# A score matmul with its own wait, one gate bank, and a last round in halves: attention on one Trainium2 core

## The chip, the core and the metric

The kernel runs on one core of one Trainium2 chip. The metric is the device time of an execution in microseconds; a time for a kernel is the median of several executions. Beside it stands one profiled execution, which records every instruction of every engine: TensorE (PE, its weight loads PEld), VectorE (DVE), ScalarE (ACT), GpSimd (POOL), and SyncE (SP), which issues most of the DMAs.

## What is computed

Two attentions over the same x of 2048 positions and 512 features, with 32 heads of 16, mixed by a gate of each position:

```python
x = A_x
g = _sigmoid((x * gate_w).sum(-1, keepdims=True))
a = _A_ref(x, A_wqkv, A_wo)      # softmax(q k^T / 4) v, then wo
b = _B_ref(x, B_wqkv, B_wo)      # phi(q) (phi(k)^T v) / (phi(q) sum phi(k)), then wo
return g * a + (1 - g) * b
```

Here phi(t) is t + 1 for positive t and exp(t) otherwise, and everything comes in bfloat16. The softmax branch is nearly all of the work: 32 x 2048 x 2048 scores, each of which needs an exponential.

## The kernel before

**A planner writes the order.** The kernel is a Python program that simulates the engines while it is built. In a loop (from L1394) it asks a set of functions for candidates (`cand_s`, `cand_pv`, `cand_op1`, `cand_exp` and so on, and the steps of the tasks), picks one by planned start, priority and a few constants (L160 to L184), and records it with `emit` (L308) or `dma` (L340). `_Eng.add` (L62) keeps, for each engine, the list of instructions with the semaphore values that they wait for. Then the lists are played into the program as they stand. So the order on each engine is fixed at build time, and a changed cost or constant can redraw all of it.

**Waits.** A group of PE instructions recorded together waits once, ahead of its first, and signals once, at its last. An instruction carries one wait itself; further ones become EventSemaphore instructions ahead of it on the same engine. The waits stand in the order in which the dependencies were listed, and the first one goes into the instruction itself.

**Scores.** The softmax branch has 32 rounds: four heads' positions at a time (t8, a query chunk of 512, and a parity), and within a round 16 key blocks by 4 row groups. One unit is one matmul of 32x128 weights with 512 queries, which fills one PSUM bank of 128x512. All 2048 come from `cand_s` (L614) or `cand_dsolo`. Banks 0 and 1, and 2 and 3, are ScalarE's two sets; banks 4 and 5 are VectorE's. A score wave is two matmuls for a set of ScalarE and mostly one for VectorE, as one group with one wait and one signal:

```python
fns = [s_fn(r, kb, j, b0 + k) for k, (r, kb, j) in enumerate(units)]
fns += [s_fn(u[0], u[1], j, bk) for _, j, u, bk in extra]
```

**Exponentials.** ScalarE takes a set with one exp of 128x1024 (L771) into one of ten slots of P. VectorE makes its exponentials by integer arithmetic: op1 (L685) writes scaled 16-bit integers to Z, from which two shifted versions are made, on POOL (L739) or VectorE (L749); read as bfloat16, the three are multiplied with three scaled copies of V.

**PV.** Waves of four matmuls (L775 on, `cand_pv`) add P or Z times V into bank 7. At a round's end `aout` (L1016) transposes bank 7 to T1 on VectorE (L1021), takes the reciprocal of the sums (L1040), multiplies it with the gate (L1042), scales (L1044), and transposes into OAT (L1048). In the last round the small steps are on VectorE.

**Other tasks** fill PE between: projections (`t_q`, `t_k`, `t_v`, whose scaled copies of V are POOL's L988), phi of k and q (exp L1056, L1057, L1058), the linear branch's sums and outputs, and `t_final` (L1172), which applies the two output matrices and writes 128 rows. PE is kept busy by matmuls on a dummy tile where nothing else is due (`fill`, L1347).

**The gate** is `t_gate` (L993). POOL spreads the gate weights over 128 columns (L994). For each of the four query chunks, four matmuls (each as four column groups, 64 in the trace) make the logits in a bank of its own, VectorE transposes it (L1002), and POOL picks a column of 16. Then ScalarE's exp, POOL's +1, VectorE's reciprocal into gt (used by L1042), POOL's 1-g (L1010), and four copies on VectorE (L1013) into gnat, which the linear branch's output uses. The spread weights share storage with T2 and the transposes with outt.

**SP's queue.** SP issues, in order, the loads of x and of the weights (wA: the softmax branch's, wB: the linear branch's), eight small DMAs for each query tile (Qz<-QT, within SBUF, L965), the transposing DMAs of the linear branch's output (xnat<-wA, L1168), and the writes of the output.

**The tail.** The last four `t_final` need the last round's OAT. Their copies out of PSUM are two on ScalarE (L1202) and two on VectorE (L1204).

Of the kernel before, what the change touches and what calls it, by code (L numbers as in the profile page):

```python
# [28 lines left out]
class _Ev:  # L29
    __slots__ = ("E", "idx")  # L30

    def __init__(self, E, idx):
        self.E = E
        self.idx = idx


class _Eng:
# [24 lines left out]
    def add(self, fn, deps=(), inc=True, dma_sem=None):  # L62
        waits = []
        for d in deps:
            if d is None:
                continue
# [8 lines left out]
            for k, (s2, v2) in enumerate(waits):  # L75
                if s2 is sem:
                    if val > v2:
                        waits[k] = (sem, val)
                    break
            else:  # L80
                waits.append((sem, val))
# [46 lines left out]
def bass_gated_mix__mha_block__linear_attn_block__prompt_kernel(  # L128
# [31 lines left out]
    FILL = 0.704  # L160
    HOT = 32.85
    BACK = 1005.06
    SHB = 4
    why = [None]
    PMIN = 2
# [3 lines left out]
    STICK = 45.888  # L169
    OPP = 400  # L170
    FDL = 60
    DENS = 0.581
    AGE = 300.0
    MZ = 0.0
    MZD = 0.0
    HOLD = 74.192
    NACT = 4
    BIAS = 141.142
    KEYW = 32.578
    PVW = 1365.46  # L180
    DTOL = 44.045
    TTOL = 38.407
    PKR, MTR, PQR, PQS, FR = 0.500, 9.56, 12.93, 1.804, 0.0
    KR, KS, QR = 7.15, 1.60, 4.00  # L184
# [5 lines left out]
    with ExitStack() as es:  # L190
# [40 lines left out]
        gwr = T2[:, 0, :].rearrange("p (c n) -> p c n", c=NCC)  # L231
# [10 lines left out]
        ge = SB([128, NQC, 16], FP32, "ge")  # L242
# [7 lines left out]
        PE = _Eng("pe", SEM("s_pe"), 150.0)  # L250
# [26 lines left out]
        r_OAT = [[R(f"OAT{t}_{q}") for q in range(NQC)] for t in range(NT8)]  # L277
        r_eb = [R(f"eb{i}") for i in range(2)]
# [8 lines left out]
        r_gt, r_ge, r_gl, r_gnat = R("gt"), R("ge"), R("gl"), R("gnat")  # L287
# [20 lines left out]
        def emit(E, dur, fns, reads=(), writes=(), name=""):  # L308
# [4 lines left out]
            fin = start + dur + E.pipe  # L313
# [5 lines left out]
            for k, fn in enumerate(fns):  # L319
                ev = E.add(fn, deps if k == 0 else (), inc=(k == len(fns) - 1))  # L320
                if first is None:
                    first = ev
# [11 lines left out]
            RLOG.append((E.name, dur, E.pipe, [(d.E.name, d.idx) if isinstance(d, _Ev) else ("dma", id(d.sem), d.val) for d in deps if d is not None],  # L334
# [3 lines left out]
        dma_eng = {}  # L338

        def dma(E, o, i, sem, total, lat, reads=(), writes=(), transpose=False, noncontig=False, name="dma", issue=60.0):  # L340
            start = max(E.free, _avail(E, reads, writes))
            E.free = start + issue
            fin = start + lat
            eng = {"sp": nc.sync, "act": nc.scalar, "pool": nc.gpsimd}[E.name]
# [47 lines left out]
        q_fill = [0] * NQZ  # L392
# [1132 lines left out]
```

The softmax here doesn't subtract the row's maximum and nothing guards it: scores larger than these inputs give would overflow.

## Time and profile before

| what | us |
|---|---|
| median of 8 executions | 681.16 |
| lowest and highest of them | 678.72, 681.62 |
| the profiled execution, device time | 680.91 |
| its span | 678.8 |
| ScalarE busy (share of the span) | 658.2 (97%) |
| PE busy | 666.1 (98%) |
| VectorE busy | 609.2 (90%) |
| POOL busy | 550.2 (81%) |

The span runs from the first to the last recorded instruction; 2.1 us of the device time lie around it. A row of the groups, for example

```profile
L739 POOL TENSOR_TENSOR Z<-Z,mcon 128x512 int32<-128x512 int32 x465 | 480.0, 1056 | 80.8 <-DVE Z L685 48.3
```

reads: line 739 of the kernel, on GpSimd, writes tile Z from Z and mcon, 465 times; 480.0 us in total, 1056 ns each; before these instructions the engine stood idle for 80.8 us, of which 48.3 ended when VectorE's L685 was done. Instructions of one engine overlap in part, so a mean duration can be longer than the time from one to the next, and the busy time of a group is the union. In the rows of the timeline, neighbouring instructions of a kind are put together with a count. The granted PE clock was full in all 40 slices.

### The profile page before, as it was taken

Reading aid. Unit: us, or ns where it says so; the run is one execution under the profiler, and the core shown is the slowest. Engines: PE = TensorE matmul, PEld = TensorE weight load, DVE = VectorE, ACT = ScalarE, POOL = GpSimd, SP = SyncE. Lnnn points to the kernel's source line nnn. Section 1 sums busy time; section 2 is a strip of 40 time slices with the busy share of each in tenths; the row PEclk is TensorE's granted clock in tenths of the full one; section 3 lists DMA queues with packets and bytes.
Section 4 is the critical chain, followed back from the end, with each engine's and each line's share of the span. In section 5 each row is a group of like instructions: output and inputs, shape, how many; then the busy total and the mean of one; then the engine's idle time right before and its main releaser. Section 6 shows DMA issues by size and latency. Waiting matters only on the chain.

```text
span 678.8 us, 24102 instructions
## 1 busy us (share of the span) xinstructions
PE 666.1 (98%) x9886; PEld 202.6 (30%) x9886; DVE 609.2 (90%) x1062; ACT 658.2 (97%) x734; POOL 550.2 (81%) x611
## 2 busy tenths in 40 slices
PE   8899999999999999999999999999999999999998
PEld 3322233323223232222333322232332332222222
DVE  6889999998899998999899888899998988899996
ACT  6799999999999999999999999999999998999995
POOL 4677879889878888888897888898788997887882
PEclk9999999999999999999999999999999999999999
DMA  6520001200000000000001000001020021000000
GB/s 128 138 88 6 5 2 20 85 8 4 2 9 2 10 2 2 10 2 2 12 3 65 10 10 1 10 15 24 7 34 9 14 47 33 17 16 11 26 17 32
DMA packets 27963, 15.96 MB, mean 24 GB/s; under 512 B 19792, under 2 KB 26832, under 8 KB 27856
## 3 DMA queue, kind: packets, MB, share of 16 engines
q1 hardware_dynamic: 26512, 13.91, 8.1%
q8 instruction: 79, 1.29, 0.8%
q10 hardware_dynamic: 1344, 0.52, 0.3%
q14 instruction: 28, 0.23, 0.1%
HBM read 6.69 MB, written 2.10 MB: 13 GB/s over the span
## 4 chain that ended last, share of the span: by engine, by line
PE 72%; ACT 14%; issue 5%; DVE 4%; SPq 3%; DMA 1%; POOL 0%; ACTq 0%; DVEq 0%
PE ps L371 56%; PE ps L377 17%; ACT P L771 13%; SPq L348 2%; DVE Z L685 2%; ACT eb L1056 1%; DMA gwc<-in_gate_w_dram 1%; DMA xnat<-wA 0%; DVE T L1021 0%; DVE gnat L1013 0%; DVE QT L957 0%; DVE wA L1163 0%; POOL Vc L988 0%; SPq L352 0%; DVE Z L749 0%
## 5 line engine op out<-in xcount | busy, mean ns | idle before, releaser
L771 ACT ACTIVATE P<-ps 128x1024 bf16<-128x1024 f32 x695 | 645.8, 1119 | 8.3 <-PE ps L371 8.1
L739 POOL TENSOR_TENSOR Z<-Z,mcon 128x512 int32<-128x512 int32 x465 | 480.0, 1056 | 80.8 <-DVE Z L685 48.3
L685 DVE TENSOR_SCALAR Z<-ps 128x512 int16<-128x512 f32 x659 | 440.9, 684 | 53.4 <-PE ps L371 45.3
L371 PE MATMUL ps<-Z,Vc 128*17 128x512 bf16 x1977 | 282.5, 382 | 0.3
L371 PE MATMUL ps<-Qz,KT 32*128 32x512 bf16 x2048 | 272.4, 385 | 3.4 <-DVE Z L685 1.0
L371 PE MATMUL ps<-P,Vc 128*17 128x512 bf16 x1389 | 250.2, 383 | 2.2 <-POOL Vc L988 2.1
L371 PEld LDWEIGHTS ps<-Qz,KT 32*128 32x128 bf16 x2048 | 68.7, 91 | 259.0 <-ACT P L771 234.9
L371 PEld LDWEIGHTS ps<-Z,Vc 128*17 128x17 bf16 x1977 | 63.9, 88 | 79.2 <-issue 52.3
L749 DVE TENSOR_SCALAR Z<-Z 128x1024 int16<-128x1024 int16 x195 | 82.5, 439 | 0.2
L371 PEld LDWEIGHTS ps<-P,Vc 128*17 128x17 bf16 x1389 | 56.3, 88 | 57.5 <-issue 40.6
L371 PE MATMUL ps<-warm 128*32 128x512 bf16 (+15 forms) x600 | 61.9, 326 | 1.2 <-DVE dummy L420 1.2
L377 PE MATMUL ps<-xT,wA 128*32 128x512 bf16 (+1 forms) x528 | 43.9, 376 | 0.7 <-DMA xT<-in_A_x_dram 0.4
L1057 POOL TENSOR_SCALAR eb<-eb 128x512 f32<-128x512 f32 x32 | 20.1, 629 | 15.6 <-ACT eb L1056 9.1
L988 POOL TENSOR_SCALAR Vc<-Vc 128x576 bf16<-128x576 bf16 x32 | 21.7, 679 | 6.2 <-DVE Vc L985 2.7
L371 PEld LDWEIGHTS ps<-warm 128*32 128x32 bf16 (+1 forms) x600 | 20.2, 95 | 18.6 <-issue 12.1
L1021 DVE STREAM_TRANSPOSE T<-ps 128x512 f32<-128x512 f32 x32 | 22.6, 707 | 2.5 <-PE ps L377 2.3
L377 PE MATMUL ps<-wA,xnat 128*32 128x512 bf16 x256 | 22.6, 382 | 1.8 <-DVE wA L1163 1.8
L1044 POOL TENSOR_TENSOR T<-T,rg 128x256 bf16<-128x256 f32 x31 | 19.5, 630 | 5.8 <-DVE Z L749 2.7
L377 PE MATMUL ps<-phiK,xnat 128*32 128x512 bf16 x256 | 23.2, 383 | 0.0
L1056 ACT ACTIVATE eb<-ps 128x512 f32<-128x512 f32 x32 | 22.6, 705 | 0.0
L377 PE MATMUL ps<-wA,OAT 128*32 128x512 bf16 x256 | 22.5, 382 | 0.0
L377 PE MATMUL ps<-wB,xT 128*32 128x512 bf16 x256 | 22.4, 382 | 0.0
(79 smaller groups left out, 277.3 us busy)
## 6 DMA issues: line engine op xcount, KB each, us to landing
Qz<-QT SPq DMA_DIRECT2D x120, 16.0 KB, 1.8
wA<-in_A_wqkv_dram SPq DMA_DIRECT2D x4, 384.0 KB, 4.2
wB<-in_B_wqkv_dram SPq DMA_DIRECT2D x4, 384.0 KB, 3.2
xnat<-in_A_x_dram SPq DMA_DIRECT2D x3, 512.0 KB, 3.8
out_dram<-outt SPq DMA_DIRECT2D x12, 128.0 KB, 1.7
wA<-in_A_wo_dram SPq DMA_DIRECT2D x1, 512.0 KB, 3.8
wA<-in_B_wo_dram SPq DMA_DIRECT2D x1, 512.0 KB, 4.8
out_dram<-wA SPq DMA_DIRECT2D x4, 128.0 KB, 1.8
```

The lines of the kernel that those rows point to most:

```text
L348: return eng.dma_start_transpose(o, i)
L371: return lambda: nc.tensor.matmul(o, lhsT=l, rhs=r, start=start, stop=stop, skip_group_check=sg)
L377: h = nc.tensor.matmul(o[32 * j:32 * j + 32], lhsT=l[:, 32 * j:32 * j + 32], rhs=r, start=start, stop=stop, skip_group_check=True)
L685: return C(DV, OPP, 533 * n + 74, lambda: nc.vector.tensor_scalar(o, i, ZB, 0.0, op0=ALU.add, op1=ALU.max), [r_bank[b] for b in bks], r_Z[ ...
L739: return C(PO, 400, 70 + 484 * n, lambda: nc.gpsimd.tensor_tensor(Z[:, z, 0:512 * n].bitcast(I32), Z[:, z0, 0:512 * n].bitcast(I32), mcon[ ...
L749: return C(DV, 450 if hot else 300, 69 + 134 * n, lambda: nc.vector.tensor_scalar(Z[:, z, 0:512 * n], Z[:, z0, 0:512 * n], float(m), None, ...
L771: return C(AC, 500, 427 * n + 49, lambda: nc.scalar.activation(P[:, slot, 0:512 * n], bank(b0, n), ACT.Exp, scale=ESC), [r_bank[b0 + k] fo ...
L988: yield po(690, lambda k=k: nc.gpsimd.tensor_scalar(Vc[:, k, vs].rearrange("p a b c -> p (a b c)"), Vc[:, 0, vs].rearrange("p a b c -> p ( ...
L1021: yield dv(607, lambda: nc.vector.transpose(T1[:, a, :], bank(7)), [r_bank[7]], [r_T1[a]])
L1044: yield E(340 if r == NR - 1 else 640, lambda k=k: (nc.vector if r == NR - 1 else nc.gpsimd).tensor_tensor(dst_[:, k], src[:, k, :, 0:16], ...
L1056: yield ac(480, lambda: nc.scalar.activation(eb[:, i, :], bank(b), ACT.Exp), [r_bank[b]], [r_eb[i]])
L1057: yield po(640, lambda: nc.gpsimd.tensor_scalar(eb[:, i, :], eb[:, i, :], 1.0 + 1e-6, 0.0, op0=ALU.min, op1=ALU.max), [r_eb[i]], [r_eb[i]])
```

## The change

Five things change.

1. In `cand_s` the VectorE matmul of a score wave is no longer in ScalarE's group. It is recorded as a group of its own directly behind (`part`), with its own waits and its own signal.
2. `add` sorts dependencies by the planned finish of what is waited for (`fin`), so that the order of the waits of an instruction changes.
3. `t_gate` makes the logits of the four query chunks in one bank: 16 matmuls instead of 64, one transpose instead of four, and an exp over 16 columns that reads the transposed tile itself. The result lies in another layout, so sixteen DMAs of 32x16 numbers bring it to gt, and four more bring 1-g to gnat in place of the four VectorE copies. The spread weights are 32 columns wide instead of 128.
4. In the last round `aout` works in two halves of 256 columns, each from the transpose of bank 7 to the transpose into OAT. Of the last four `t_final`, two depend on the first half and two on the second. Three of their copies are on ScalarE and one on VectorE.
5. The planner's constants have other values, and the planner counts a time for each DMA in SP's queue (1100 ns for a transposing one, 590 for a Qz one, 300 for any other).

In the order that comes out, PE has 9802 matmuls instead of 9886 (48 of them the gate's; the rest are fills), ScalarE 693 exps of 128x1024 instead of 694 and one half, VectorE 662 op1 instead of 659, and SP 201 DMAs instead of 181. On SP the sixteen gate DMAs stand behind four loads of wA and the first of wB, and ahead of the first two blocks of Qz and the other three loads of wB. The diff, with declarations left out:

```diff
@@ -61,9 +62,7 @@
         waits = []
-        for d in deps:
-            if d is None:
-                continue
+        for d in sorted([d for d in deps if d is not None], key=lambda d: d.fin if isinstance(d, _Ev) else 0.0):
             if isinstance(d, _Raw):
...
@@ -74,11 +73,10 @@
                 if s2 is sem:
-                    if val > v2:
-                        waits[k] = (sem, val)
+                    val = max(val, v2)
+                    del waits[k]
                     break
-            else:
-                waits.append((sem, val))
+            waits.append((sem, val))
         self.n += 1
...
@@ -157,31 +155,33 @@
-    FILL = 0.704
+    FILL = 0.711
...
-    BACK = 1005.06
-    SHB = 4
+    BACK = 980.186
+    SHB = 3
...
-    PMIN = 2
+    PMIN = 3
...
-    STICK = 45.888
+    STICK = 65.578
...
-    DENS = 0.581
+    DENS = 0.598
...
+    PEP = 148.771
+    PVD = 216
...
-    HOLD = 74.192
+    HOLD = 109.508
...
-    BIAS = 141.142
-    KEYW = 32.578
-    PVW = 1365.46
-    DTOL = 44.045
+    BIAS = 120.045
+    KEYW = 39.753
+    PVW = 685.579
+    DTOL = 114.55
...
-    PKR, MTR, PQR, PQS, FR = 0.500, 9.56, 12.93, 1.804, 0.0
-    KR, KS, QR = 7.15, 1.60, 4.00
+    PKR, MTR, PQR, PQS, FR = 0.404, 9.56, 12.93, 1.667, 0.0
+    KR, KS, QR = 7.15, 1.48, 4.00
...
@@ -305,12 +307,12 @@
 
-        def emit(E, dur, fns, reads=(), writes=(), name=""):
+        def emit(E, dur, fns, reads=(), writes=(), name="", more=0.0):
             if callable(fns):
...
             E.free = start + dur
-            fin = start + dur + E.pipe
+            fin = start + dur + E.pipe + more
             deps = deps_of(E, reads, writes)
...
@@ -583,10 +591,11 @@
         class C:
-            __slots__ = ("E", "prio", "dur", "fns", "reads", "writes", "after", "name", "mode", "wt", "lock", "task")
+            __slots__ = ("E", "prio", "dur", "fns", "reads", "writes", "after", "name", "mode", "wt", "lock", "task", "part")
 
...
                 self.task = task
+                self.part = None
                 self.wt = wt
...
@@ -627,10 +636,13 @@
             n = len(units)
-            reads = s_reads(units + [(u[0], u[1], j) for _, j, u, _ in extra])
+            reads = s_reads(units)
             fns = [s_fn(r, kb, j, b0 + k) for k, (r, kb, j) in enumerate(units)]
-            fns += [s_fn(u[0], u[1], j, bk) for _, j, u, bk in extra]
-            writes = writes[:n] + [r_bank[x[3]] for x in extra]
+            part = None
+            if extra:
+                part = (216.0, [s_fn(u[0], u[1], j, bk) for _, j, u, bk in extra], s_reads([(u[0], u[1], j) for _, j, u, _ in extra]),
+                        [r_bank[x[3]] for x in extra], "Dsolo" + "".join(f"+D{x[2]}{x[1]}" for x in extra))
+            writes = writes[:n]
 
...
@@ -644,8 +656,9 @@
             STATS.setdefault('sn', {})
-            return C(PE, 1000, 222, fns, reads, writes, after, f"S{units}" + "".join(f"+D{x[2]}{x[1]}" for x in extra), "row",
-                     0.25 * (n + len(extra)))
+            c = C(PE, 1000, 222, fns, reads, writes, after, f"S{units}", "row", 0.25 * (n + len(extra)))
+            c.part = part
+            return c
 
...
@@ -991,26 +1004,33 @@
-            yield po(900, lambda: nc.gpsimd.tensor_copy(gwr, gwc[:].unsqueeze(2).to_broadcast([128, NCC, 128])), [r_gw], [r_gwr])
-            yield ("WAIT", lambda: ("x", 0) in flags and phi_free[0])
-            phi_free[0] = False
+            yield po(400, lambda: nc.gpsimd.tensor_copy(gwr, gwc[:].unsqueeze(2).to_broadcast([128, NCC, 32])), [r_gw], [r_gwr])
+            yield ("WAIT", lambda: all(("x", t) in flags for t in range(NQC)))
+            b = yield ("BANK",)
+
+            def g4(cc):
+                def go():
+                    for j in range(4):
+                        h = nc.tensor.matmul(bank(b)[32 * j:32 * j + 32], lhsT=gwr[:, cc, :], rhs=xT[:, cc, 512 * j:512 * (j + 1)],
+                                             start=(cc == 0), stop=(cc == NCC - 1), skip_group_check=True)
+                    return h
+                return go
+            for h in range(2):
+                yield pe_step(2, 512, [g4(2 * h), g4(2 * h + 1)], [*[r_xT[t][h] for t in range(NQC)], r_gwr], [r_bank[b]])
+            yield dv(607, lambda: nc.vector.transpose(gl, bank(b)), [r_bank[b]], [r_gl, *r_outt])
+            yield ("FREE", b)
+            yield ac(230, lambda: nc.scalar.activation(ge[:, 0, :], gl.rearrange("p (a b) -> p a b", b=32)[:, :, 0], ACT.Exp, scale=-1.0),
+                     [r_gl, *r_outt], [r_ge])
+            yield po(150, lambda: nc.gpsimd.tensor_scalar(ge[:, 1, :], ge[:, 0, :], 1.0, None, op0=ALU.add), [r_ge], [r_ge])
+            yield dv(170, lambda: nc.vector.reciprocal(ge[:, 0, :], ge[:, 1, :]), [r_ge], [r_ge])
...
-                b = yield ("BANK",)
-                for h in range(2):
-                    yield pe_step(2, 512, [mmt(bank(b), gwr[:, cc, :], xT[:, cc, 512 * qc:512 * (qc + 1)], start=(cc == 0), stop=(cc == NCC - 1))
-                                           for cc in (2 * h, 2 * h + 1)], [r_xT[qc][h], r_gwr], [r_bank[b]])
-                yield dv(607, lambda b=b: nc.vector.transpose(gl, bank(b)), [r_bank[b]], [r_gl, *r_outt])
-                yield ("FREE", b)
-                yield po(250, lambda qc=qc: nc.gpsimd.tensor_copy(ge[:, qc, :], gl.rearrange("p (a b) -> p a b", b=32)[:, :, 0]),
-                         [r_gl, *r_outt], [r_ge])
-            phi_free[0] = True
-            yield ac(300, lambda: nc.scalar.activation(gt[:], ge[:], ACT.Exp, scale=-1.0), [r_ge], [r_gt])
-            yield po(200, lambda: nc.gpsimd.tensor_scalar(ge[:], gt[:], 1.0, None, op0=ALU.add), [r_gt], [r_ge])
-            yield dv(650, lambda: nc.vector.reciprocal(gt[:], ge[:]), [r_ge], [r_gt])
-            yield po(200, lambda: nc.gpsimd.tensor_scalar(ge[:], gt[:], -1.0, 1.0, op0=ALU.mult, op1=ALU.add), [r_gt], [r_ge])
+                for a in range(4):
+                    yield ("DMA", gt[32 * a:32 * (a + 1), qc, :], ge[32 * qc:32 * (qc + 1), 0, :], semGN, 256, 2500.0, [r_ge], [r_gt], False,
+                           qc == 0 and a == 0)
+            yield po(200, lambda: nc.gpsimd.tensor_scalar(gp[:], gt[:].rearrange("p q (c a) -> p a (q c)", a=4), -1.0, 1.0, op0=ALU.mult, op1=ALU.add),
+                     [r_gt], [r_gp])
...
-                src = ge[32 * a:32 * (a + 1), :, :].rearrange("p q (c a2) -> p (q c) a2", a2=4)[:, :, a]
-                yield dv(150, lambda a=a, src=src: nc.vector.tensor_copy(gnat[32 * a:32 * (a + 1), :], src), [r_ge], [r_gnat])
+                yield ("DMA", gnat[32 * a:32 * (a + 1), :], gp[32 * a:32 * (a + 1), a, :], semGP, 64, 2500.0, [r_gp], [r_gnat], False, a == 0)
...
@@ -1018,10 +1038,16 @@
-            yield dv(607, lambda: nc.vector.transpose(T1[:, a, :], bank(7)), [r_bank[7]], [r_T1[a]])
+            def tr_half(hf):
+                cs = slice(256 * hf, 256 * (hf + 1))
+                return dv(341, lambda: nc.vector.transpose(T1[:, a, cs], bank(7)[:, cs]), [r_bank[7]], [r_T1[a]])
+            if r == NR - 1:
+                yield tr_half(0)
+            else:
+                yield dv(607, lambda: nc.vector.transpose(T1[:, a, :], bank(7)), [r_bank[7]], [r_T1[a]])
...
-                st["acc_free"] = True
+                st["acc_free"] = r < NR - 1
...
@@ -1031,6 +1057,20 @@
+            if r == NR - 1:
+                for hf in range(2):
+                    cs, gs = slice(256 * hf, 256 * (hf + 1)), slice(8 * hf, 8 * (hf + 1))
+                    if hf:
+                        yield tr_half(1)
+                    sv = T1[:, 1, cs].rearrange("p (q d) -> p q d", d=32)
+                    yield dv(115, lambda sv=sv, gs=gs: nc.vector.reciprocal(rec[:, 1, gs], sv[:, :, 16]), [r_T1[1]], [r_rec[1]])
+                    yield dv(70, lambda gs=gs: nc.vector.tensor_tensor(rg[:, c, 1, gs], rec[:, 1, gs], gt[:, qc, gs], ALU.mult), [r_rec[1], r_gt], [r_rg[c]])
+                    yield dv(210, lambda sv=sv, gs=gs, cs=cs: nc.vector.tensor_tensor(
+                        T2[:, c, cs].rearrange("p (q h d) -> p h q d", h=2, d=16)[:, 1], sv[:, :, 0:16],
+                        rg[:, c, 1, gs].unsqueeze(2).to_broadcast([128, 8, 16]), ALU.mult), [r_T1[1], r_rg[c]], [r_T2[c]])
+                    yield dv(341, lambda cs=cs: nc.vector.transpose(OAT[:, t8, 512 * qc:512 * (qc + 1)][:, cs], T2[:, c, cs]), [r_T2[c]], [r_OATL[hf]])
+                    yield ("FLAG", lambda hf=hf: flags.add(("oatl", hf)))
+                return
...
@@ -1038,10 +1078,9 @@
             yield dv(155 + 17 * n, lambda: nc.vector.reciprocal(rc, src[:, :, :, 16]), rT1, rr)
-            E = dv if r == NR - 1 else po
-            yield E(70 if r == NR - 1 else 230 + 25 * n, lambda: (nc.vector if r == NR - 1 else nc.gpsimd).tensor_tensor(rgc, rc, gv, ALU.mult), [*rr, r_gt], rrg)
+            yield po(230 + 25 * n, lambda: nc.gpsimd.tensor_tensor(rgc, rc, gv, ALU.mult), [*rr, r_gt], rrg)
             for k in range(n):
-                yield E(340 if r == NR - 1 else 640, lambda k=k: (nc.vector if r == NR - 1 else nc.gpsimd).tensor_tensor(
+                yield po(640, lambda k=k: nc.gpsimd.tensor_tensor(
                     dst_[:, k], src[:, k, :, 0:16], rgc[:, k].unsqueeze(2).to_broadcast([128, 16, 16]), ALU.mult),
...
@@ -1185,10 +1224,10 @@
-                return [r_xn[qb], r_woB] if kind == "b" else [r_OAT[i][qc], r_woA]
+                return [r_xn[qb], r_woB] if kind == "b" else [r_OATL[qbl // 2] if tail and i == NT8 - 1 else r_OAT[i][qc], r_woA]
...
-            yield ("WAIT", lambda: ("oat", NT8 - 1, qc) in flags)
+            yield ("WAIT", lambda: (("oatl", qbl // 2) if tail else ("oat", NT8 - 1, qc)) in flags)
...
@@ -1198,7 +1237,7 @@
                 yield ("WAIT", lambda: qb < 2 or ("f", qb - 2) in flags)
-            if tail and qbl % 2 == 1:
+            if tail and qbl != 2:
                 yield ac(480, lambda: nc.scalar.copy(ot, bank(b)), [r_bank[b]], [r_ot])
...
@@ -1450,13 +1489,17 @@
-                fin = dma(SP, o, i, sem, tot, lat, reads=rd, writes=c.writes, transpose=tr, name=c.name)
+                fin = dma(SP, o, i, sem, tot, lat, reads=rd, writes=c.writes, transpose=tr, name=c.name, occ=1100.0 if tr else 590.0 if c.name[0] == 'Q' else 300.0)
...
-                fin = emit(c.E, c.dur, c.fns, c.reads, c.writes, name=c.name)
+                if c.part:
+                    emit(PE, 6.0, c.fns, c.reads, c.writes, name=c.name, more=c.dur - 6.0)
+                    fin = emit(PE, c.part[0], *c.part[1:4], name=c.part[4])
+                else:
+                    fin = emit(c.E, c.dur, c.fns, c.reads, c.writes, name=c.name)
```

## The prediction

> **What bounds the kernel now.** I read the busy shares first, then the groups by line and form, then the waits, and then walked the timeline along every gap of ScalarE.
>
> ```profile
> PE 666.1 (98%) x9886; PEld 202.6 (30%) x9886; DVE 609.2 (90%) x1062; ACT 658.2 (97%) x734; POOL 550.2 (81%) x611
> ...
> L771 ACT ACTIVATE P<-ps 128x1024 bf16<-128x1024 f32 x694 | 645.3, 1120 | 8.3 <-PE ps L371 8.1
> L685 DVE TENSOR_SCALAR Z<-ps 128x512 int16<-128x512 f32 x659 | 440.9, 684 | 53.4 <-PE ps L371 45.3
> ```
>
> PE has the larger share, but its ends are modelled and part of its work is filling (600 matmuls on `warm`), so its 98% says little. ScalarE is the bound: 694 exps of 128x1024 with 8.3 us idle before them in the whole span. Their durations (1120 ns) overlap; what counts is from one end to the next, 917 ns in the steady stretches. 694 x 0.917 is 636 us, and the 32 exps of the linear branch (L1056) add 0.49 each. What exceeds 917 ns sums to about 10.2 us, and that is all a better order can win, unless exps go away.
>
> ```profile
> PEld ps L371 <- ACT P L771: 238.0, 602, 1.2
> ...
> ACT P L771 <- PE ps L371: 8.1, 7, 4.1
> ...
> PEld ps L371 <- DVE Z L685: 13.9, 55, 0.5
> ```
>
> These are waits: total us, times, longest. PE waits for the exp to free its banks 602 times: the loop is exp, score matmuls, exp, with ScalarE last. Only 55 times does the score wave end its wait on VectorE. ScalarE waits on PE 7 times, 4.1 us in one of them.
>
> The 10.2 us, found on the timeline (start, duration, and in brackets the idle time before):
>
> ```profile
> 23.40 0.61 POOL L994 COPY T<-gwc 128x512 bf16<-128x512 bf16 x1 [2.75 <-DMA gwc<-in_gate_w_dram]
> ...
> 25.67 0.40 PE L371 MATMUL ps<-P,Vc 128*17 128x512 bf16 x4 [2.06 <-POOL Vc L988]
> ...
> 26.12 4.03 ACT L771 ACTIVATE P<-ps 128x1024 bf16<-128x1024 f32 x4 [4.05 <-PE ps L371]
> ```
>
> The gate's weight copy waits for its DMA, POOL's Vc scaling is behind it, PE's PV wave behind that, the exp behind that: 4.9 us at 21 to 27 us.
>
> ```profile
> 64.06 2.13 DVE L1013 COPY gnat<-ge 32x16 f32<-32x16 f32 x4
> ...
> 67.27 0.40 PE L371 MATMUL ps<-Qz,KT 32*128 32x512 bf16 x3 [1.03 <-DVE Z L685]
> ```
>
> Four gate copies hold VectorE 2.1 us; the score wave then waits for its bank, and the exp at 67.70 is 0.86 late. A third place is 562 us: 1.9 us, behind the transposes that follow eight Qz DMAs on the SP queue (551.8 to 557.5). Two small ones at 36 and 39 us (0.54, 0.29) stand beside the gate's matmuls; the start costs 0.6, the rest is spread.
>
> ```profile
> 36.70 5.58 SPq L352 DMA_DIRECT2D Qz<-QT  x8
> 42.32 0.58 SPq L352 DMA_DIRECT2D wB<-in_B_wqkv_dram  x1
> 43.23 2.41 SPq L352 DMA_DIRECT2D Qz<-QT  x4
> 45.68 0.58 SPq L352 DMA_DIRECT2D wB<-in_B_wqkv_dram  x1
> ```
>
> This is SP's queue. One SBUF to SBUF DMA takes 0.51 to 0.59 us to issue, 0.63 from one to the next (5.58 for 8 with hiccups); loads from DRAM 0.33 after idle, 0.43 to 0.58 behind others. SP is in order, so a block of small DMAs delays what stands behind it.
>
> **What the Trainium skill says.** "DMA: Bandwidth & Descriptors", section "Issuing engines are not separate DMA queues", says that the sequencer's time to initiate a DMA is usually small relative to the DMA itself. The trace agrees for one (0.6 of 1.8 us to landing), but a run of sixteen is not small. "Perfetto Trace Analysis", section "Identifying Dependency Chains", says that an instruction with several waits may have EventSemaphore instructions ahead of it; the trace has them: a score weight load starts 41 ns after the exp's signal when it waits itself, 105 ns when an EventSemaphore does. "TensorE: Matmul & The Clock Gate", section "The cost: per-tile semaphore tail", prices an extra signal at about 26 ns; the change has some 620 more signals, but on PE, which has slack in most waves.
>
> **The change part by part**, against the profiled execution's own 680.91 us (span 678.8 and 2.1 around it; the median is 681.16, 0.25 more).
>
> *Split of the score wave.* PE's EventSemaphores fall from 580 to 86, signals rise from 2357 to about 2974. The gain is where VectorE's bank comes free after ScalarE's: about 40 of 695 waves, mostly by 0.1 to 0.4 us, and ScalarE has about 0.15 us of slack. At most 1 us; I take -0.5.
>
> *Waits in order of their planned end.* In the new program the exp's EventSemaphore takes PE's signal and the ACTIVATE an older one; before it was the other way round. By PE's numbers this adds some 50 ns where the scores are just in time. Exps with less than 50 ns of slack: 48 of 694; so at most 1.6 us if the 158 loosely tight ones don't count, 5.3 if they do, nothing if the sequencer looks ahead. I take +0.9.
>
> *Exps.* 693 full instead of 694 and a half: 1.5 x 0.917 = -1.4, VectorE takes three more units (659 to 662) in 70 us of its own idle time. Certain, if VectorE is never the last.
>
> *Gate, what goes.* The weight copy writes 128x128 instead of 128x512 (0.61 us): -0.45 at 23 us, the DMA wait before it stays. 64 gate matmuls become 16, four transposes (711 ns) one, four POOL copies go, and so do the four gnat copies: the stalls of 0.54, 0.29, 0.86 and about 0.2 beside them, -1.9. The gate's exp stands elsewhere: +0.2.
>
> *Gate, what comes.* Sixteen gt DMAs and four gnat DMAs on SP. In the new order SP issues: four wA, one wB, the 16 gt (behind the gate's reciprocal, about 35.0 us by the steady period), eight Qz, two wB, eight Qz, the last wB, then gnat. With i the time from one gt to the next, SP leaves them at 35.0+16i; 16 Qz at 0.66 (10.6) and two wB at 0.6 put the last wB's issue at 47.0+16i; 3.4 us to landing (3.15 to 3.65 in the trace) gives 50.4+16i. The first phi_k matmuls wait for it, and stand on PE ahead of the score wave of exp 47: with their 16 matmuls, the wave and the exp that one ends at 52.7+16i. Undisturbed it ends at 56.5. So the stall is X = 16i-3.8. In the kernel before the same wait is first met at 71 us, with the load landed at 49.3; here it is met at about 54. POOL's op on gt stands ahead of one Z shift for 2 to 3 us of the same time, which lies inside X.
>
> The trace has no DMA of 2 KB between SBUF parts. From below: 0.34 (a load on an idle queue), X = 1.6. From above: 0.63, the Qz row's repeat, X = 6.3. Qz is the only one with both ends in SBUF, and nothing behind a busy queue was repeated below 0.47, so I take 0.63: **+6.3**.
>
> *562 us.* The eight Qz now have one transposing DMA behind them instead of seven: -1.9. What is late next is the next exp's own period.
>
> *Last round in halves.* Before, the path from the last accumulation:
>
> ```profile
> 671.52 0.72 DVE L1021 STREAM_TRANSPOSE T<-ps 128x512 f32<-128x512 f32 x1 [2.27 <-PE ps L377]
> ...
> 674.00 1.20 PEld L377 LDWEIGHTS ps<-wA,OAT 128*32 128x32 bf16 x28 [0.42 <-DVE OAT L1048]
> ...
> 675.75 0.58 ACT L1202 CAST wA<-ps 128x512 bf16<-128x512 f32 x1 [0.49 <-PE ps L377]
> ```
>
> VectorE needs 2.48 us from the transpose's start to PE's. By halves (each step at half its elements plus the fixed part seen in 128x16) the first half is ready after 1.75, the second after 3.46. Then ten matmul waves in all are on PE, five of them after the second half instead of seven, and three copies on ScalarE of 0.49 apart instead of two: the last ends 4.78 after the transpose's start instead of 4.23. One wave less after the last exp (-0.2), rest of the rounding of it: +0.2, between -0.2 and +0.6.
>
> *Everything else the constants move.* Small stalls outside those named are about 1.1 us now; the redrawn plan may have 0.6 to 3: +0.5.
>
> Sum: -0.5 +0.9 -1.4 -0.45 -1.9 +0.2 +6.3 -1.9 +0.2 +0.5 = **+1.95**, 682.8 us.
>
> **Rivals.** First, the other side, faster: the gt DMAs issue like loads on a quiet queue, 0.34 to 0.40. Place: SP's queue from 35 us; price 16i; it decides below i = 0.51, where X falls to the 4.35 us that the rest wins. Then X is 1.6 to 2.6 and the time 678.1 to 679.2. For it: they are 2 KB against Qz's 16, and both 128 and 512 KB loads on an idle queue take 0.33 to 0.45. Against: the repeat of 0.63 in the only row of the kind.
>
> Second, no difference: i between 0.47 and 0.55, X 3.7 to 5.0, 680.3 to 681.6. For it: wA's loads repeat in 0.47 behind each other.
>
> Third, a wait in place of the one removed: the exps' EventSemaphore costs its 50 ns at all 158 exps with little slack, 5.3 instead of 0.9, on top of X: 687. Against: ScalarE's steady period also holds an EventSemaphore before.
>
> That VectorE becomes the bound (90% busy, three units more) I don't see: it would show first as waits of PE on L685, now 13.9 us in all.
>
> **How the numbers follow.** Likeliest case 0.41, first rival 0.32, second 0.20, third 0.07. 0.2% is 1.36 us, about what a measurement of this kernel can tell from no change. Faster is the first rival, 0.32; the same is the second, 0.20; slower the rest, 0.48. The forecast's own range is 681.8 to 684.5 (X from 5.5 to 6.5, unknowns of 1 us). The range for 8 in 10 takes in the first rival from 678.4 and leaves the third out: 678.4 to 685.2.
>
> **What would show it.** SP's timeline: 16 `gt<-ge` issues from about 35 us, over about 10 us by the forecast, under 6.5 by the first rival; the last wB behind them at about 57. ScalarE: one idle stretch of 4 to 7 us between 45 and 65 us, with PE behind a wB DMA; none at 67 and 562; the one at 26 us shorter by half a microsecond. L771 x693, and the total of its idle time above 8.3. Steady stretches at 917 ns as before: if they grow, the third rival. The prediction is wrong if there is no such stall between 45 and 65 us, or if the plan has a new one where I saw none.

## The result, and the profile after

The changed kernel takes 685.43 us (median of 11, 683.53 to 687.31); the kernel before, run beside it, 681.0. The ratio is 1.0072, with a 95% interval of 1.0059 to 1.0084. It is slower, by about 4.4 us (4.9 by the ratio); the prediction had 682.8 us and a range to 685.2. The profiled execution took 685.06 us with a span of 682.9, against 680.91 and 678.8.

The page of the changed kernel, and its waits (total us, times, longest us):

```profile
PE 668.6 (98%) x9802; PEld 203.5 (30%) x9802; DVE 604.1 (88%) x1059; ACT 658.5 (96%) x733; POOL 549.1 (80%) x612
...
L784 ACT ACTIVATE P<-ps 128x1024 bf16<-128x1024 f32 x693 | 644.4, 1089 | 12.0 <-PE ps L377 11.5
```

```profile
PEld ps L377 <- ACT P L784: 244.2, 612, 0.8
...
PEld ps L377 <- DVE Z L698: 11.5, 48, 0.6
...
ACT P L784 <- PE ps L377: 11.5, 12, 3.4
```

ScalarE is still the bound, with one exp fewer and the same busy time. Its idle time before the exps grew from 8.3 to 12.0 us, and twelve waits on PE make nearly all of it. The exps' ends in both traces say where. Every 128x1024 exp ends 917 ns after the one before it if nothing is late, and every exp of the linear branch 490; what exceeds that, by stretch of the profiled executions:

| stretch, us | before | changed | what it is |
|---|---|---|---|
| to 30 | 4.9 | 2.3 | the gate's weight copy behind its DMA |
| 30 to 45 | 0.8 | 0.6 | gate |
| 45 to 63.3 | 0.2 | 7.9 | two stalls, below |
| 63.3 to 70 | 0.9 | 1.1 | before: the gnat copies; changed: below |
| 70 to 550 | 0.5 | 2.0 | small late exps |
| 550 to 575 | 2.0 | 0.1 | the transposes behind Qz |

The first exp ended 0.6 us later in the changed profile, the two exps saved (one full, and one half) give back 1.4, and the tail differs by 0.1 (8.2 and 8.3 us from the end of the last exp to the end of the span).

The two stalls. The tile gt takes the gate, and gp is 1-g, which POOL makes from gt. First SP's queue in the changed kernel (start, duration, DMAs):

```profile
33.74 10.75 SPq L358 DMA_DIRECT2D gt<-ge  x16
44.53 5.01 SPq L358 DMA_DIRECT2D Qz<-QT  x8
49.59 2.08 SPq L358 DMA_DIRECT2D wB<-in_B_wqkv_dram  x2
...
56.69 0.58 SPq L358 DMA_DIRECT2D wB<-in_B_wqkv_dram  x1
```

Then the timeline of the other engines, with the idle time before in brackets:

```profile
45.73 0.30 POOL L1030 TENSOR_SCALAR gp<-gt 128x64 f32<-128x64 f32 x1 [4.00 <-DMA gt<-ge]
...
47.08 0.39 PE L377 MATMUL ps<-Z,Vc 128*17 128x512 bf16 x1 [2.79 <-POOL Z L752]
...
47.90 1.94 ACT L784 ACTIVATE P<-ps 128x1024 bf16<-128x1024 f32 x2 [2.67 <-PE ps L377]
```

```profile
57.02 0.39 PE L377 MATMUL ps<-Qz,KT 32*128 32x512 bf16 x3
...
60.08 0.62 PE L383 MATMUL ps<-wB,xT 128*32 128x512 bf16 x4 [2.67 <-DMA wB<-in_B_wqkv_dram]
...
61.48 0.61 PE L377 MATMUL ps<-Qz,KT 32*128 32x512 bf16 x3
...
62.19 1.02 ACT L784 ACTIVATE P<-ps 128x1024 bf16<-128x1024 f32 x1 [3.40 <-PE ps L377]
```

Sixteen gate DMAs hold SP for 10.8 us. POOL's op on their result waits 4.0 us, PE waits behind POOL, the exp behind PE. Then the last load of wB leaves at 56.69, and PE waits for it until 60.08. And each stall is followed by a slower PE: the same three score matmuls take 0.39 us at 57.02 and 0.61 at 61.48. The windows (us, then busy time of each engine and count, then the granted clock as a share of full speed, DMA share, GB/s) show the clock:

```profile
55.00:60.00 5.00, 2.39 (x53) 0.94 (x45) 3.17 (x5) 3.79 (x5) 4.60 (x7) 0.89 0.33 93
60.00:65.00 5.00, 4.92 (x38) 1.01 (x38) 1.95 (x3) 2.54 (x3) 1.47 (x2) 0.50 0.02 4
```

From 60 to 65 us PE is busy, at half the clock. The trace's own record of the clock has it at half from 48.6 to 52.1 us, from 1.5 us after PE came back from the first pause, and from 58.9 to 65.7 us, beginning within the second.

### The profile page after: what moved, and what is told of

Read it like the earlier page. It is cut to its first block, busy times and chain, and to the rows that moved or that the text cites. A ratio compares the mean times of both kernels' runs of the same rounds, so it can differ in the third digit from the quotient of the medians.

```text
span 682.9 us, 23420 instructions
## 1 busy us (share of the span) xinstructions
PE 668.6 (98%) x9802; PEld 203.5 (30%) x9802; DVE 604.1 (88%) x1059; ACT 658.5 (96%) x733; POOL 549.1 (80%) x612
## 4 chain that ended last, share of the span: by engine, by line
PE 81%; ACT 10%; issue 3%; SPq 2%; DVE 1%; DMA 1%; POOL 1%; POOLq 0%; DVEq 0%; ACTq 0%
PE ps L377 64%; PE ps L383 17%; ACT P L784 10%; SPq L354 2%; DVE Z L698 1%; DMA gwc<-in_gate_w_dram 1%; DMA wB<-in_B_wqkv_dram 0%; POOL Z L752 0%; SPq L358 0%; POOL Vc L1001 0%; ACT eb L1095 0%; DVE T L1047 0%; PE ps L1014 0%; DVE QT L970 0%; ACT wA L1241 0%
## 5 line engine op out<-in xcount | busy, mean ns | idle before, releaser
L377 PE MATMUL ps<-Z,Vc 128*17 128x512 bf16 x1986 | 288.1, 384 | 3.1 <-POOL Z L752 2.8
L377 PE MATMUL ps<-Qz,KT 32*128 32x512 bf16 x2048 | 278.8, 386 | 3.2 <-ACT P L784 0.7
L377 PE MATMUL ps<-P,Vc 128*17 128x512 bf16 x1386 | 247.3, 385 | 0.7 <-POOL Vc L1001 0.5
L762 DVE TENSOR_SCALAR Z<-Z 128x1024 int16<-128x1024 int16 x192 | 79.1, 428 | 0.0
L377 PE MATMUL ps<-warm 128*32 128x512 bf16 (+15 forms) x558 | 56.2, 321 | 1.3 <-DVE dummy L428 1.2
L383 PE MATMUL ps<-xT,wA 128*32 128x512 bf16 (+1 forms) x528 | 42.5, 380 | 0.1
L383 PE MATMUL ps<-wB,xT 128*32 128x512 bf16 x256 | 24.6, 397 | 2.7 <-DMA wB<-in_B_wqkv_dram 2.7
L377 PEld LDWEIGHTS ps<-warm 128*32 128x32 bf16 (+1 forms) x558 | 18.0, 96 | 15.3 <-issue 9.4
L383 PE MATMUL ps<-xT,wB 128*32 128x512 bf16 x256 | 22.1, 383 | 0.0
```

The source lines that it names most:

```text
L377: return lambda: nc.tensor.matmul(o, lhsT=l, rhs=r, start=start, stop=stop, skip_group_check=sg)
L383: h = nc.tensor.matmul(o[32 * j:32 * j + 32], lhsT=l[:, 32 * j:32 * j + 32], rhs=r, start=start, stop=stop, skip_group_check=True)
L762: return C(DV, 450 if hot else 300, 69 + 134 * n, lambda: nc.vector.tensor_scalar(Z[:, z, 0:512 * n], Z[:, z0, 0:512 * n], float(m), None, ...
```

## The experiments

All are the changed kernel, or the one before, with the order that its planner drew and only the named edits in the lists or their waits, so that no plan is redrawn. The first diffs give the lists in short. Each run was timed against the kernel before on the same chip, in five rounds. The medians differ from set to set by some tenths of a us (the kernel before: 680.8, 681.43 and 681.19 in the three sets), so ratios are given; 0.1% is 0.68 us.

**wB's loads between the gate DMAs.**

```diff
-SP: gt x16, Qz x8, wB x2, Qz x8, wB
+SP: gt, wB, gt x5, wB, gt x6, wB, gt x4, Qz x16
```

> The changed kernel, only SP's queue differs: three of wB's loads stand between the sixteen gate DMAs (behind the 1st, 6th and 12th) instead of behind them and two blocks of Qz. Theory (SP's queue): the loads land before 45 us, PE's 2.7 us wait on wB at 57 us goes, and so does the slow stretch of PE's clock behind it (1.1 us of late exps); the gate DMAs end 1.9 us later, so POOL's wait on them and PE's wait behind it grow from 2.8 to about 4.7 us. Net about -3.5 us: 682, against 685.4. Rival (the stalls are incidental, the loss is in the order of waits and the redrawn plan): no change beyond 0.5 us.

684.47 us, ratio 1.0045 (1.003 to 1.006). PE no longer waits for wB, and one stall is left, longer: the exp at 49.96 us has 4.56 us of idle time before it, and two late ones follow at half clock. The stalls are as expected; the time is not. It fell by 1.0 us by the medians, 2.4 by the profiled executions, where 3.5 were expected. The profiled one had a single stretch of PE at half clock (mean granted clock 0.997); six of the eight had 0.992 to 0.995, about as low as the changed kernel's, so part of the gain was lost to the clock again, at places that no trace shows.

**gp eight POOL ops later.**

```diff
-POOL: gp, Z shift x8
+POOL: Z shift x8, gp
```

> The changed kernel, only POOL's order differs: the op that reads the sixteen gate DMAs' result (gp) stands eight shifts later. Theory (SP's queue, and wB's landing is a fixed point in time): PE's 2.8 us wait at 44 us goes, the exps run ahead, and then wait for the same wB landing at 60.1 us, so all of it is given back there: 684.5 to 686. Rival (the two stalls add): -4.3 us with the slow clock behind the first, 681.

685.87 us, ratio 1.0063 (1.0044 to 1.0082), as the theory had it. ScalarE in that run:

```profile
54.80 1.02 ACT L784 ACTIVATE P<-ps 128x1024 bf16<-128x1024 f32 x1 [2.52 <-PE ps L377]
...
63.56 1.02 ACT L784 ACTIVATE P<-ps 128x1024 bf16<-128x1024 f32 x1 [3.81 <-PE ps L377]
```

The stall at 47.90 is gone; the exps run on to 52 us and then stop for 2.5 us, and again for 3.8. PE's wait behind the first of these is a new one:

```profile
53.20 0.39 PE L377 MATMUL ps<-Qz,KT 32*128 32x512 bf16 x1 [2.25 <-DMA Qz<-QT]
```

The first block of Qz stands behind the sixteen DMAs too. The second stop is PE's wait for wB, now 2.96 us, until 61.45. Removing the first wait won nothing: what stands behind the same DMAs on SP took it back.

**Both edits.**

> Both edits together: wB's loads between the gate DMAs, and gp eight shifts later. Theory (SP's queue): no stall of PE between 40 and 66 us, exps at 917 ns through, no slow clock: -9 us against the changed kernel, 676.5, which is below the kernel before by about 4.5. Rival (the loss is in the order of waits and the redrawn plan): 684 to 685.4. If the sixteen DMAs cost in another way (the SBUF ports, say), between.

683.67 us, ratio 1.0047 (1.0032 to 1.0062): the expectation failed by 7 us. PE in that run:

```profile
54.13 0.60 PE L377 MATMUL ps<-Qz,KT 32*128 32x512 bf16 x1 [3.74 <-DMA Qz<-QT]
```

With the other two readers out of the way, the third is alone: PE needs the first block of Qz at 50.4 us, and the wait that was 2.25 us in the run with gp later is 3.74 here, where that block leaves SP behind wB's loads as well. The result lies next to the rival's, but not for the rival's reason.

**PE kept busy in the waits.**

```diff
+PE: 40 matmuls of zeros into bank 7
 PE: Z,Vc (waits for POOL)
...
+PE: 40 matmuls of zeros into bank 7
 PE: wB,xT (waits for wB)
```

> The changed kernel with 40 matmuls of zeros (ten waves of four) added to bank 7 ahead of each of the two PE instructions that wait, so that PE works for about 2.2 us of each wait. No wait is shortened. If the falling clock of an idle PE is part of the loss: the granted clock stays at full between 45 and 70 us, the exps behind the second stall come at 917 ns, and the time falls by 1.1 to 2 us to about 683.8; what it wins behind the first stall is taken by the wB wait. If the clock has no part: 685.4 or slightly more.

684.88 us, ratio 1.005 (1.0035 to 1.0066). The window that stood at half clock:

```profile
60.00:65.00 5.00, 4.12 (x49) 1.17 (x49) 2.77 (x6) 2.92 (x4) 0.61 (x1) 1.00 0.05 15
```

The clock is full, and behind the wait for wB the exps come at their 917 ns, where the changed kernel lost another 1.1 us. What it won behind the first stall lengthened the second (4.16 us of idle time instead of 3.40). The gain is 0.6 us by the medians, 1.5 by the ratios, whose intervals overlap. So the windows show that the slow clock comes with the stall and goes when PE is kept busy; what it costs is known only roughly.

**Qz first, then the gate DMAs.**

```diff
-SP: gt x16, Qz x8, wB x2, Qz x8, wB
+SP: Qz x8, wB x2, gt x2, wB, gt x14, Qz x8
-POOL: gp, 11 ops
+POOL: 11 ops, gp
```

> The third run showed the next link of the chain: with wB's loads and gp out of the way, PE waited 3.7 us for the first block of Qz, which stands behind the same sixteen DMAs. Here SP issues that block and two of wB's loads first, then two gate DMAs, the last wB, the other fourteen, and gp stands eleven POOL ops later; nothing else of the changed kernel differs. Theory (SP's queue, three readers behind one block of DMAs): no wait of PE on a DMA or on gp between 40 and 66 us, granted clock full there, about -8.5 us against the changed kernel's 685.4: 676.5 to 677.5, below the kernel before (680.8) by 3 to 4. Rival (something else bounds those 25 us, a fourth reader or POOL): again one stall of 4 to 5 us in another place, 682 to 684.

677.23 us, ratio 0.9937 (0.9919 to 0.9956). SP and ScalarE in that run:

```profile
34.15 5.54 SPq L358 DMA_DIRECT2D Qz<-QT  x8
39.74 1.17 SPq L358 DMA_DIRECT2D wB<-in_B_wqkv_dram  x2
40.95 1.15 SPq L358 DMA_DIRECT2D gt<-ge  x2
42.15 0.58 SPq L358 DMA_DIRECT2D wB<-in_B_wqkv_dram  x1
42.77 9.79 SPq L358 DMA_DIRECT2D gt<-ge  x14
```

```profile
39.44 15.74 ACT L784 ACTIVATE P<-ps 128x1024 bf16<-128x1024 f32 x17
55.01 0.66 ACT L1095 ACTIVATE eb<-ps 128x512 f32<-128x512 f32 x1
```

Seventeen exps without a gap. The same DMAs, as many and as slow, now cost ScalarE nothing, because nothing that is due soon stands behind them. This is 8.2 us under the changed kernel by the medians, 9.2 by the ratios, and 4.2 below the kernel before. The mean granted clock was 1.000 in all six executions; in the changed kernel's it was 0.990 to 0.997.

**Four gate DMAs instead of sixteen**, in the changed kernel's own order.

```diff
-gt[32a:32a+32, qc] <- ge[32qc:32qc+32]   (16 DMAs of 32x16)
+gt[:, qc] <- ge[:, 0]                    (4 DMAs of 128x16)
```

> The changed kernel in its own order, but four gate DMAs of 128x16 numbers in place of the sixteen of 32x16 (left out: the replication over the four groups of partitions, so that gt has other numbers). Twelve issues of 0.634 less: SP is 7.6 us earlier with everything behind. Theory (the price is the number of issues): gp, the first Qz block (landed at about 43.5) and the last wB (about 52.5) all come in time, no stall, 676.5 to 677.5 as in the run before it in this set. Rival (the price is in the bytes or the landing of these DMAs, not in the issues): still stalls of 3 us or more, 680 or above.

677.26 us, ratio 0.994 (0.9921 to 0.9958), the same as in the run before. SP:

```profile
34.61 2.57 SPq L1510 DMA_DIRECT2D gt<-ge  x4
37.22 5.50 SPq L358 DMA_DIRECT2D Qz<-QT  x8
...
50.04 0.58 SPq L358 DMA_DIRECT2D wB<-in_B_wqkv_dram  x1
```

As many bytes in a quarter of the DMAs take 2.57 us instead of 10.75: the price is per issue.

**The order of waits undone.** On top of the Qz-first kernel, `add` takes the dependencies in the old order.

```diff
-for d in sorted([d for d in deps if d is not None], key=lambda d: d.fin if isinstance(d, _Ev) else 0.0):
+for d in deps:
```

> As the first run of this set (Qz before the gate DMAs, gp later), and the waits of an instruction stand in the old order again, not sorted by planned finish, so that the exp waits on PE's signal itself. Theory (the sorted order costs an exp that comes just in time about 60 ns: 84 ns from PE's signal to its start in the changed trace, 23 in the trace of before): the small late exps spread from 100 to 630 us, 2.2 us in all in the changed kernel, shrink; -0.7 to -2.3 us against the first run of this set. Rival (the sequencer hides it or the sorted order wins as much on PE): within 0.5 us.

675.49 us, ratio 0.9915 (0.9896 to 0.9934): 1.7 us less than with the sorted order by the medians. The two intervals just meet, but the clock was full in all executions of both, and only one of six here took longer than the shortest of six there. From the trace, 31 exps ended more than 8 ns late in the Qz-first kernel and 12 here; between 70 and 550 us they lose 1.0 us instead of 1.9.

**The split undone.** On top of the Qz-first kernel with its sorted waits, the wait of VectorE's score matmul goes to the head of ScalarE's group.

> As the first run of this set, and the wait of VectorE's score matmul stands on ScalarE's group again, ahead of both (the signals stay two). Theory of the prediction (the split wins where VectorE's bank is late): +0.3 to +1 us against the first run of this set. Rival (it wins nothing, as ScalarE has slack there): within 0.3 us.

681.4 us, ratio 1.0004 (0.9993 to 1.0014): 4.2 us more, four times the upper end of what I expected. The waits of the Qz-first kernel, and of this one:

```profile
PEld ps L377 <- ACT P L784: 247.2, 621, 0.8
PEld ps L377 <- issue: 116.8, 509, 0.6
```

```profile
PEld ps L377 <- issue: 206.9, 734, 0.8
PEld ps L377 <- ACT P L784: 80.8, 200, 0.8
```

421 waits on the exp are gone from the list, and "issue" has 225 more: in these waves the weight load no longer waits for the exp itself. An EventSemaphore ahead of it does, and this view does not draw that as a wait. The programs say why: sorted by planned finish, the exp's signal comes last in the list, and all but the first of a list go into EventSemaphores. By the program it is there in 424 waves, and the trace has 416. In 109 of these the load starts 100 to 109 ns after the exp's signal, and in none sooner; in the kernel before, where the load waits itself, 115 start 40 to 49 ns after it.

**Split and order undone.**

> As the run with the split undone (Qz before the gate DMAs, gp later, VectorE's wait on ScalarE's group), and the waits in the old order too. In the run with the split undone alone, the sorted order had put the exp's signal, mostly the last to come, into an EventSemaphore ahead of 424 score waves; here the score matmul waits on the exp itself and the EventSemaphore holds VectorE's, in 497 waves, as in the kernel before. Theory (the 4.2 us of that run are the price of the sorted order on a joint wait, not of VectorE's late banks): 0.2 to 1 us above the run with the order alone undone (0.9915 of the kernel before), 0.992 to 0.993. Rival (VectorE's banks are late in this plan, which was drawn for a split wait): 4 us above it, 0.997 to 0.998.

676.3 us, ratio 0.9927 (0.9915 to 0.9939), 0.8 us above the run with the order alone undone. So the 4.2 us were the sorted order's, on a joint wait. The split itself may be worth about 0.8 us in this plan: the small late exps between 70 and 550 us add 0.6 in the trace, but the intervals of the two runs overlap, so this is not shown.

**The kernel before with sorted waits**, and nothing else.

> The kernel before, its order of instructions untouched, only the waits of each instruction sorted by planned finish. Then 685 exps wait on PE through an EventSemaphore and 429 score waves on the exp through one. Theory (each costs 60 ns where it comes last): as much as undoing the split cost in the changed kernel, plus the exps' share: +4 to +6 us, 685.5 to 687. Rival (the order of waits costs nothing much where no split is): within 1 us of the kernel before.

684.93 us, ratio 1.0055 (1.0042 to 1.0068): +3.7 us, just below what was expected, with the same mark (waits on ScalarE 602 before, 200 here):

```profile
PEld ps L370 <- issue: 200.8, 714, 0.6
PEld ps L370 <- ACT P L770: 76.8, 200, 0.6
```

**The kernel before with the split**, and nothing else.

> The kernel before, its order untouched, only VectorE's score matmul with its own wait and signal behind ScalarE's in 503 waves (EventSemaphores on PE from 580 to 82). Theory of the prediction: -0.5 us, between 0 and -1, as about 40 waves end their wait on VectorE and ScalarE has 0.15 us of slack. Rival (the split is worth what undoing it cost, 4 us): -3 to -4.

681.3 us, ratio 1.0002 (0.9992 to 1.0012). Nothing, or less than a measurement can tell; nor do the 633 more signals on PE show in the time, which would be 16 us if each held the exps up by the 26 ns that the prediction names. Compared at the same granted clock (0.997 in ten executions of each), the split kernel is 0.2 us faster in the mean, so a gain of half a microsecond is neither shown nor excluded.

**The weight copy behind Vc**, on top of the run with the old order of waits.

> As the run with the order alone undone (Qz before the gate DMAs, gp later, old order of waits), and POOL's copy of the gate weights stands behind the two Vc scalings instead of ahead of them. In its trace the copy waits for its DMA until 22.78 us, the two scalings run at 23.16, PE's PV wave at 24.64, and the exp at 25.08 is 1.82 us late; Vc is ready on VectorE at 22.28. Theory (the copy's DMA is what the exp waits for): the scalings start at 22.3, that exp is 0.8 to 0.9 us earlier, and so is the end: -0.8 us. Rival (the wait moves to the gate's matmuls at 31 us): no change.

674.85 us, ratio 0.9907 (0.9894 to 0.9921), 0.6 below; the intervals overlap. The late exp of that place has 0.92 us of idle time before it instead of 1.71, about as expected. It starts at 23.57 instead of 25.08 us, but half of that is the first exp of this profile, which came 0.7 us sooner:

```profile
23.57 3.77 ACT L787 ACTIVATE P<-ps 128x1024 bf16<-128x1024 f32 x4 [0.92 <-PE ps L380]
```

This is the fastest version found: the changed kernel with Qz ahead of the gate DMAs, gp and the weight copy later on POOL, and the waits in their old order. It is about 6 us below the kernel before and 10 below the changed one.

## Why the prediction was wrong

The direction and the place were right, the size was not: 1.6 to 2 us were forecast, 4.4 came.

- **The price of a gate DMA** was taken as 0.63 us from one to the next, from Qz's row. In the trace it is 0.63, with one of 1.27. The last wB was to leave at 57.1 and left at 56.69, to land by 60.5 and was there at 60.08; exp 47 (the 47th of 128x1024) was to end at 62.8 and ended at 63.2. The first rival, with issues of 0.34 to 0.40, is refuted, and so is the second.
- **The failed step is the size of X**, "the stall is X = 16i-3.8", put at 6.3 us. The Qz-first run is the changed kernel without it, and 8.2 us faster. Side by side, the two traces give 8.7 (spans 8.9 apart, 0.2 of it before the first exp's end). All of this stretch came earlier than forecast: the first gate DMA left at 33.74 us and not at 35.0, and exp 47 undisturbed ends at 55.4 (55.2 in the Qz-first run, with the first exps laid on each other) and not at 56.5. So the parts are compared by their lengths:

  | part of X, us | forecast | measured |
  |---|---|---|
  | first gate DMA to the last wB load's issue | 22.1 | 22.95 |
  | from there to its landing | 3.4 | 3.4 |
  | landing to the end of exp 47 | 2.3 | 3.1 |
  | lost again up to exp 53 | no term | 0.9 |
  | less: first gate DMA to the undisturbed end of exp 47 | 21.5 | 21.7 |
  | X | 6.3 | 8.7 |

  The queue was slower by 0.85 us: one gate DMA held SP for 1.23 us and one wB load for 1.45. (The forecast's own terms sum to 46.8+16i, where it wrote 47.0.) The third and fourth rows, 1.7 us together, are PE at half clock, and they are the larger part of what was missing. The prediction had no term for the clock: it priced a stall of PE as its own length.
- **The chain has three readers.** I named wB as the wait, and put POOL's wait inside it; the first Qz block, the third, I had only as work of the queue. It is hidden in the changed kernel and comes out as soon as gp is out of the way. That POOL's wait adds nothing of its own was right: what is gained ahead of wB's landing is waited away there, as the run with gp later shows. The 8.2 us are the price of the three together.
- **All else.** Without X the prediction's terms sum to -4.35 us. The Qz-first run, in which X is gone and all the rest of the change stays, is 4.2 us below the kernel before. That the two agree is in part luck. The prediction priced a profiled execution at full clock, and most recorded executions of the kernel before have a stretch at half clock (see the last section). And its terms were off both ways:
- **The split**: -0.5 forecast, nothing measured in the kernel before (1.0002), perhaps -0.8 in the changed plan, which is not shown.
- **The order of waits**: +0.9 forecast, with 5.3 as the upper end. 1.7 measured with the split, 3.7 in the kernel before without it. The step looked at the exps' side alone. On PE the same sort puts the exp's signal behind VectorE's, and there nearly every wave has it last; the split hides this, as a group with one wait has no order. The two parts of the change were treated as independent and are not.
- **562 us**: -1.9 forecast, -2.0 in the trace; the gap is gone.
- **The weight copy**: -0.45 forecast. In the two profiles the exps up to 30 us lose 2.6 us less, but the stall there varies by 2.2 us between profiles of the old order (last section), so the term is neither confirmed nor refuted.
- **The gate's old stalls** at 36, 39 and 67 us: the one at 67 is gone in the Qz-first run, as forecast (in the changed kernel the slow clock stands in its place). Between 30 and 45 us the exps lose only 0.2 us less, where 0.8 was forecast. Of the -1.9 in all, about -1.1 came.
- **The exps**: -1.4, as forecast (693 against 694 and a half). **The tail**: +0.2 forecast, +0.1 measured. The halves are ready 1.77 and 3.35 us after the start of the first transpose (forecast 1.75 and 3.46). The forecast's 4.78 for the end of ScalarE's last copy rests on a misreading: in the kernel before that copy starts 4.23 us after the transpose's start and ends at 4.81. In the changed kernel it starts at 4.71 and ends at 5.30.
- **Small late exps** between 70 and 550 us: 0.5 before, 2.0 after; with the old order of waits 1.0. So the redrawn plan adds about 0.5 in these single profiles, the forecast's +0.5.
- **Not foreseen and not settled**: the first exp ended 0.6 us later in the changed profile. It starts between 8.6 and 9.3 us in three profiles of the old plan and between 9.0 and 10.0 in those of the new, so part of it may be chance, and no run was made for it.
- The third rival (an EventSemaphore at each exp) had the mechanism of the order of waits, but its steady stretches stay at 917 ns in all traces.

## What to carry to other kernels

Price a block of small DMAs by issues times the repeat of the queue, and then list everything that stands behind it on that queue with the time at which it is due: the first wait hides the others, and here removing it alone won nothing. A wait of PE can cost more than its length, as its clock may fall. If an instruction has several waits, see which one sits in the instruction and which in an EventSemaphore, and let the one that comes last in time be in the instruction. A gain ahead of a wait with a fixed end is no gain.

## What the runs showed of the hardware

- **PE's clock after a pause.** In the changed kernel PE's clock fell to half around two pauses of 2.79 and 2.67 us without a matmul, for 3.5 and 6.8 us. In all runs, ahead of the last exp, a stretch at half clock lasted 3.4 to 3.5 us or 6.8 to 6.9. The length of the pause alone does not decide: there was no fall after 2.06 and 1.84 us in the kernel before (at 25.67 and 561.58 us), and there was one after 1.24 us in the kernel before with sorted waits (at 563.76 us). The Trainium skill ("TensorE: Matmul & The Clock Gate", section "HAM oscillation — how this bites in real kernels") gives the rule of no idle gap above about 3.4 us; here shorter ones were enough. With zeros in the pauses the clock stayed full.
- **The same kernel with and without such a stretch.** Of the 66 executions of the kernel before that ran beside the experiments, 24 had a mean granted clock of 1.000 and took 679.9 us on average, 40 had 0.997 and took 681.7. Half clock for 3.4 us makes about that difference in the mean clock. The profiled execution of the kernel before is one with a full clock. In the profile of the kernel before with the split, which is not, the stretch lies from 561.8 to 565.2 us, behind the wait at 562 us, and the exps lose 3.7 us there instead of 2.0. That it lies there in the kernel before too is likely, and not shown.
- **An EventSemaphore costs up to about 60 ns** where its signal comes last. An exp starts 23 ns after PE's signal when it waits itself; in the changed kernel, where an EventSemaphore waits, seven of the late exps start 49 or 50 ns after it and five 83 or 84, and in the kernel before with sorted waits most start 82 or 83 after it. A score weight load starts after 41 ns when it waits itself and 105 when an EventSemaphore does.
- **A small DMA between SBUF parts cost SP the same at both sizes**: 0.59 us for 2 KB as for 16 KB. One of the sixteen took 1.23 us, and nothing shows why.
- **The wait for the gate's weights varies**: in three profiles of the old order (before, sorted, split) the late exp at 21 to 27 us lost 4.2, 2.0 and 2.7 us. A single profile prices such a stall only to a microsecond or two.
